# Pooled attention and a top-1 expert layer on one core: batches 1 to 3's keys turned in pairs, the loop's head left unaligned, half blocks' weights split in three parts

## The chip, the cores and the metric

The kernel runs on 1 core of a Trainium2 chip. The metric is the device time of one execution in microseconds (us). Of the kernel before, three timed runs are shown; the profile is of a fourth execution.

## The reference

```python
def _attn_ref(q, k, v):                      # 8 batches, 8 heads, 576 rows, 64 columns
    k_p = k.reshape(B, H, Sp, pool, D).mean(axis=3)      # 576 keys pooled by 8: 72
    v_p = v.reshape(B, H, Sp, pool, D).mean(axis=3)
    scores = scale * np.matmul(q, k_p.transpose(0, 1, 3, 2))
    ...
    return np.matmul(attn, v_p)              # attn: softmax of the scores

def _moe_ref(x, w_gate, w1, w2):             # x: 4608 tokens of 512, from attention
    expert_idx = np.argmax(x @ w_gate, axis=1)           # 8 experts, the best one
    ...
    for e in range(E):                       # w1[e]: 512 x 1024, w2[e]: 1024 x 512
        h = np.maximum(x_sorted[lo:hi] @ w1[e], 0.0)
        y_sorted[lo:hi] = h @ w2[e]
    return gate_w[:, None] * y_sorted[inv_perm]
```

## The kernel before

**Attention.** For each batch, keys and values are loaded as 5 chunks of 128 pooled rows x 512 columns (the fifth has 64 rows; the 512 are 8 neighbouring rows of 64). Three adds halve the columns to 512, 256, 128 and 64 (`pool`, L327; POOL's instructions are at L331, L333 and L335). PE turns the pooled keys (`k_pe`), and they are scaled into the tile `bd`, once in partitions 0 to 63 and once in 64 to 127 (`half`), since a query pair takes both halves of PE's rows. How the upper half is filled differs by batch. For batches 0 to 2 (`b < TWICE`) the last add is done on DVE and writes every chunk's 64 columns twice, side by side (`doubled`, L323; `kp` is then a part of the tile `both`), so that one turn gives both halves, and ACT copies the lower, DVE the upper (`two`, L383). From batch 3 on, POOL does the last add, PE turns 64 columns a chunk, ACT fills the lower half, and a DMA on SP's queue copies it to the upper (`moves`, issued at L1050). The queries are taken in 36 units; `put(i, place, step)` hangs steps into unit i at a named place, and each engine runs its steps in the order in which this program writes them. After every few units, tokens are routed: POOL scatters them by expert into the DRAM tensor `x_by_expert` (L691).

**Weights.** Each expert's float32 weights are split into a high and a low float16 part in eight pieces (0 to 3 of `w1`, 4 to 7 of `w2`): ACT rounds the high part (`wsplit`, L118), DVE makes the low part from both (L120). The first expert's pieces are split during units 12 to 32, the low parts of it in units 23 to 31.

**Expert loop.** Tokens go in blocks of up to 256 of one expert: 22 blocks with these inputs. Block 0 is done ahead of the loop; the loop runs blocks 1 to 21. A block of at most 128 rows runs half the columns (`full` false): blocks 4, 6, 11, 15 and 21. Its code is one of four copies of `block` (two weight buffers, full or half), chosen by branches in `either`. The body on PE: the products with w1 (`up_part`, `up`, L987 to L996), then those with w2 (`finish`, L1080), 24 products of 512 columns for each 128 rows. In the first block of an expert (`en` is 1: blocks 1, 4, 5, 7, 8, 12 and 15), ACT and DVE also split the next expert's eight pieces into the other weight buffer (`part`, L1277). Ahead of that stands `split_x` (L891): it splits a later block's rows, which the loop has loaded from `x_by_expert`, and waits for POOL's `keep_ids` (L872 to L877), which waits for these rows. SP's queue then runs `trans` (a DMA that turns the rows, L906), `load_x` (rows of the block three ahead, L1219) and `wwhole` (the weights of later experts, L91), in this order. The loop is written with PE's code for its head aligned to the start of a page of instructions (`head_align_engines=[ENG.PE]`).

## Time and profile before

| | us |
|---|---|
| median of 3 runs (lowest, highest) | 592.79 (590.35, 593.44) |
| the profiled execution | 594.33 |
| its span, first to last instruction | 592.5 |
| PE busy | 567.3 (96%) |
| DVE, ACT, POOL busy | 284.6, 277.9, 264.5 |

The profiled execution lies 1.54 us above the median. PE works through 96% of the span, so the table's other engines matter only where PE waits for one of them. Attention takes about the first 160 us; the loop begins at about 190. Rows give times in us from the span's start.

### The profile page before, as it was taken

What the parts mean: (1) busy time and instruction counts of PE and PEld (TensorE: products, weight loads), DVE (VectorE), ACT (ScalarE), POOL (GpSimd) and SP (SyncE); (2) the same over time, 40 slices, a digit from 0 to 9 for tenths busy, and PEclk for the clock granted to TensorE, in tenths of its full rate; (3) what the DMA queues carried; (4) which work ended last, traced back from release to release, by engine and by line L of the source; (5) the groups of instructions that cost most, each with busy time, mean ns of one, the idle gap of its engine ahead of it and who ended that gap; (6) DMA issues with size and microseconds to landing.
All of it is one profiled execution on the core that took longest, in us unless ns stands there. A gap on an engine that the chain in (4) does not pass through costs nothing. (4 is left out here: it accounts for less than half of the span.)

```text
span 592.5 us, 15080 instructions
## 1 busy us (share of the span) xinstructions
PE 567.3 (96%) x4384; PEld 422.6 (71%) x4385; DVE 284.6 (48%) x575; ACT 277.9 (47%) x625; POOL 264.5 (45%) x526
## 2 busy tenths in 40 slices
PE   8989899999998989998998999999999999999995
PEld 8888899989884765766674676676765667657763
DVE  6776466688864272228724751326512551133022
ACT  3767788889731262236735641236412642122122
POOL 5779989987964641133320433140420142201212
PEclk9999999999999999999999999999999999999998
DMA  9999998956694859636995888233142322420200
GB/s 268 300 311 287 333 327 257 318 215 203 186 307 151 236 139 394 225 90 190 270 309 112 298 253 280 53 95 82 45 111 57 83 69 85 111 59 32 71 18 34
DMA packets 96583, 107.61 MB, mean 182 GB/s; under 512 B 54502, under 2 KB 64742, under 8 KB 96552
## 3 DMA queue, kind: packets, MB, share of 16 engines
q1 hardware_dynamic: 89832, 85.93, 51.1%
q0 software_dynamic: 6720, 21.28, 9.4%
q8 instruction: 17, 0.28, 0.2%
q14 instruction: 14, 0.11, 0.1%
HBM read 73.65 MB, written 23.37 MB: 164 GB/s over the span
## 5 line engine op out<-in xcount | busy, mean ns | idle before, releaser
L1080 PEld LDWEIGHTS <-bd 128*128 128x128 f16 x936 | 91.3, 98 | 105.6
L1074 DVE SCALAR_TENSOR_TENSOR bd<-ps,bd 128x512 f16<-128x512 f32 (+1 forms) x44 | 27.6, 630 | 178.0 <-ACT bd L1071 173.7
L1242 POOL TENSOR_TENSOR spacer<-ql,iG 1x1 f32<-1x1 f32 x44 | 21.5, 489 | 188.8 <-ACT ql L1238 185.9
L515 ACT ACTIVATE both<-ps,nmx 128x72 f32<-128x72 f32 x288 | 69.1, 343 | 6.9 <-DVE nmx L508 6.7
L1071 ACT ACTIVATE bd<-ps 128x512 f16<-128x512 f32 (+1 forms) x44 | 24.1, 549 | 91.9 <-PE L996 66.0
L541 PE MATMUL po<-vb,pt 128*128 128x146 f32 (+3 forms) x400 | 57.7, 305 | 1.4 <-ACT pt L527 1.1
L1080 PE MATMUL po<-w,bd 128*128 128x512 f16 x264 | 58.9, 379 | 0.0
L1080 PE MATMUL po<-kv,bd 128*128 128x512 f16 x264 | 58.8, 379 | 0.0
L1243 POOL DMA_INDIRECT out_dram<-ql,iG x44 | 45.4, 1033 | 21.3 <-issue 20.2
L996 PEld LDWEIGHTS <-qt 128*128 128x128 f16 x528 | 47.7, 98 | 8.8 <-issue 1.8
L541 PEld LDWEIGHTS po<-vb,pt 128*128 128x128 f32 (+1 forms) x400 | 50.5, 177 | 4.8 <-ACT pt L527 3.3
L996 PEld LDWEIGHTS <-w 128*128 128x128 f16 x480 | 40.8, 98 | 14.9 <-ACT w L118 5.8
L1080 PE MATMUL pq<-kv,bd 128*128 128x512 f16 x216 | 48.1, 379 | 0.0
L498 PE MATMUL ps<-bd,qT 128*128 128x144 f32 x256 | 43.6, 294 | 4.1 <-ACT both L515 2.5
L1080 PE MATMUL pq<-w,bd 128*128 128x512 f16 x192 | 42.9, 379 | 0.0
L1238 ACT ACTIVATE ql<-po,gB 128x512 f32<-128x512 f32 x22 | 15.0, 684 | 57.1 <-PE L996 37.1
L691 POOL DMA_INDIRECT x_by_expert<-both,rpos x36 | 36.3, 1009 | 10.4 <-issue 4.9
L498 PEld LDWEIGHTS ps<-bd,qT 128*128 128x128 f32 x256 | 35.0, 190 | 6.0 <-ACT both L515 3.5
L508 DVE TENSOR_REDUCE nmx<-ps 128x4 f32<-128x288 f32 x72 | 32.0, 451 | 9.9 <-PE ps L498 9.6
L331 POOL TENSOR_TENSOR st<-kv 128x1280 f32<-128x1280 f32 x12 | 34.9, 2909 | 3.9 <-DMA kv<-in_k_dram 2.6
L895 DVE TENSOR_TENSOR bd<-vb,bd 128x1024 f16<-128x1024 f32 x22 | 27.0, 1225 | 20.1 <-issue 10.6
L527 ACT ACTIVATE pt<-pp 128x640 f32<-128x640 f32 x36 | 25.6, 710 | 20.3 <-PE pp L522 14.5
(244 smaller groups left out, 1190.3 us busy)
## 6 DMA issues: line engine op xcount, KB each, us to landing
both<-in_moe_w_dram SPq DMA_DIRECT2D x6, 2048.0 KB, 11.6
st<-in_moe_w_dram SPq DMA_DIRECT2D x6, 2048.0 KB
vb<-x_by_expert SPq DMA_DIRECT2D x16, 578.0 KB
kv<-in_v_dram SPq DMA_DIRECT2D x16, 512.0 KB
st<-in_moe_w_dram SPq DMA_DIRECT2D x8, 1024.0 KB
kv<-in_k_dram SPq DMA_DIRECT2D x6, 1024.0 KB
qt<-in_q_dram SPq DMA_DIRECT2D x6, 1024.0 KB
kv<-in_k_dram SPq DMA_DIRECT2D x4, 512.0 KB
```

Source lines behind the costliest of these rows:

```text
L331: nc.gpsimd.tensor_tensor(t1, src[:, :, 0:4 * D], src[:, :, 4 * D:], op=OP.add)
L498: nc.tensor.matmul(ps[:, x * 2 * KP:(x + 1) * 2 * KP], t[:, h, :], BD[b % 3][:, :, h, :], start=True, stop=True)
L508: nc.vector.tensor_reduce(nmx, ps[:, 0:4 * KP].rearrange("p (h x) -> p h x", x=KP), axis=AX.X, op=OP.min)
L515: nc.scalar.activation(p[:, PCOL[h]:PCOL[h] + KP], ps[:, x * KP:(x + 1) * KP], AF.Exp, bias=nmx[:, x:x + 1], scale=-1.0)
L527: nc.scalar.activation(pt, pp[:, 0:640], AF.Copy)
L541: nc.tensor.matmul(po.rearrange("p a x -> p (a x)")[m, cols], pt[:, c * 128 + m.start:c * 128 + m.stop], VB[(b + s) % 3][:, c, SLOTS[c][0] ...
L691: st = nc.gpsimd.indirect_dma_start(out=xs, out_offset=bass.IndirectOffsetOnAxis(ap=Z["pos"][:, u:u + 1], axis=0), in_=X[:, u, :], in_offs ...
L895: nc.vector.tensor_tensor(col(xh[:, :, 1]), row(xg), col(xh[:, :, 0]), op=OP.subtract)
L996: nc.tensor.matmul(dst, W1[s][z][:, d, c], xT[:, x, 0:n], start=(z == 0 and x == 0), stop=(z == 1 and d == DC - 1))
L1074: V.scalar_tensor_tensor(pair(hT[1], k, n), ups_of(k, n), 0.0, pair(hT[0], k, n), op0=OP.max, op1=OP.subtract)
L1080: nc.tensor.matmul(y, hT[x][:, f, 128 * j:128 * j + 128], W2[s][z][:, f, :], start=(half == x == z == f == 0), stop=(half == z == 1 and f ...
L1243: st = nc.gpsimd.indirect_dma_start(out=out, out_offset=bass.IndirectOffsetOnAxis(ap=iG[:, j:j + 1], axis=0), in_=ys[j], in_offset=None, b ...
```

## The change

It has four parts.

1. Keys. `kp` gets six chunk columns; the sixth is a copy of chunk 0. For batches 1 to 3, PE turns two neighbouring chunks at a time (`pair`): the lower 64 partitions of a result hold chunk c, the upper 64 chunk c+1. ACT copies the lower half to its columns, DVE the upper to columns that begin 128 further (`high`, 64x448), and the pair of chunk 4 and the copy gives the first 128. `doubled` goes: for batch 2, POOL does the last add; for batch 1, DVE does it in thirds, writing 64 columns instead of 128. Batch 3's DMA from half to half goes, and its last chunk is turned with the values (`v_pe`). For batches 2 to 7, POOL makes the copy (128x64).
2. The loop's head is no longer aligned on PE.
3. In half blocks, pieces 0 and 1 are split after the first half of the w1 products in program order, 2 and 3 after `arrive`, both ahead of `split_x`, and 4 to 7 behind it. Each of the three stands under an If of its own.
4. The low parts of the first expert's pieces are made in two DVE steps of 128x512 each, the second one place of the units later.

```diff
@@ -104,6 +104,15 @@
         nc.sync.dma_start(dst, src.rearrange("e p c f -> p (e c) f"))
 
     last_pool = []
+
+    def wsplit_low(s, i, z):
+        if i < 4:
+            c = slice(z * F // 2, (z + 1) * F // 2)
+            src, h, l = (x[..., c] for x in (ST[0][0][i // 2][:, i % 2, :], W1[s][0][:, i, :], W1[s][1][:, i, :]))
+        else:
+            j = 2 * (i - 4) + z
+            src, h, l = ST[0][1][j // 4][:, j % 4, :], W2[s][0][:, j, :], W2[s][1][:, j, :]
+        nc.vector.scalar_tensor_tensor(l, src, SW, h, op0=OP.mult, op1=OP.subtract)
 
     def wsplit(s, i, what="hl", stage=0):
         s1, s2 = ST[stage]
...
@@ -311,28 +320,29 @@
-    TWICE = 3
-
-    def pool_short(src, dst, twice=False):
+    TWICE = 4
+
+    def pool_short(src, dst, two_sums=False):
         for c in (slice(0, 2), slice(2, 4), slice(4, 5)):
             nc.gpsimd.tensor_tensor(t1[:, c], src[:, c, 0:4 * D], src[:, c, 4 * D:], op=OP.add)
-            nc.gpsimd.tensor_tensor((t3 if twice else t2)[:, c], t1[:, c, 0:2 * D], t1[:, c, 2 * D:], op=OP.add)
-            if not twice:
+            nc.gpsimd.tensor_tensor((t3 if two_sums else t2)[:, c], t1[:, c, 0:2 * D], t1[:, c, 2 * D:], op=OP.add)
+            if not two_sums:
                 nc.gpsimd.tensor_tensor(dst[:, c], t2[:, c, 0:D], t2[:, c, D:], op=OP.add)
 
-    def doubled(c=slice(0, 5)):
-        n = c.stop - c.start
-        nc.vector.tensor_tensor(kp[:, c], t3[:, c, None, 0:D].to_broadcast([128, n, 2, D]),
-                                t3[:, c, None, D:].to_broadcast([128, n, 2, D]), op=OP.add)
+    def thirds(c):
+        nc.vector.tensor_tensor(KVS["kp", 1][:, c], t3[:, c, 0:D], t3[:, c, D:], op=OP.add)
+        if c.start == 0:
+            nc.vector.tensor_tensor(KVS["kp", 1][:, 5], t3[:, 0, 0:D], t3[:, 0, D:], op=OP.add)
 
     def pool(src, dst, what=(0, 1)):
         last_pool[:] = []
         if 0 in what:
             nc.gpsimd.tensor_tensor(t1, src[:, :, 0:4 * D], src[:, :, 4 * D:], op=OP.add)
         if 1 in what:
-            nc.gpsimd.tensor_tensor(t3 if dst is kp else t2, t1[:, :, 0:2 * D], t1[:, :, 2 * D:], op=OP.add)
-            if dst is not kp:
-                nc.gpsimd.tensor_tensor(dst, t2[:, :, 0:D], t2[:, :, D:], op=OP.add)
+            nc.gpsimd.tensor_tensor(t2, t1[:, :, 0:2 * D], t1[:, :, 2 * D:], op=OP.add)
+            nc.gpsimd.tensor_tensor(dst[:, 0:5], t2[:, :, 0:D], t2[:, :, D:], op=OP.add)
+            if dst.shape[1] == 6:
+                nc.gpsimd.tensor_tensor(dst[:, 5], t2[:, 0, 0:D], t2[:, 0, D:], op=OP.add)
 
     def pool_now(src, dst, part):
         p1 = pbig[:, 0:1280].rearrange("p (c x) -> p c x", c=5)
...
@@ -348,10 +358,8 @@
     def pool_k(b, part):
-        if b < TWICE:
-            KVS["kp", b] = kp
-        elif part == 0:
-            KVS["kp", b] = work.tile([128, 5, D], F32, name="kp", bufs=2)
+        if part == 0:
+            KVS["kp", b] = work.tile([128, 6, D], F32, name="kp", bufs=2)
         pool(kv[(2 * b) % 3], KVS["kp", b], (part,))
...
@@ -362,38 +370,47 @@
     def half(b, s):
         return BD[b % 3][64 * s:64 * s + 64, s].rearrange("p h x -> p (h x)")
 
-    WITH_K = (1, 2, 3)
+    ALONE = (1, 2)
 
     def k_pe(b):
         kp = KVS["kp", b]
-        m = 128 if b < TWICE else 64
+        pm = KVS["pk", b] = psA.tile([128, 512], F32, name="pq", bufs=2)
+        if b >= TWICE:
+            for c in range(4):
+                nc.tensor.transpose(pm[0:64, c * 128:(c + 1) * 128], kp[:, c], ident)
+            return
+        for c in range(4):
+            pair(kp, c, pm[:, c * 128:(c + 1) * 128])
+        if b in ALONE:
+            KVS["p4", b] = psA.tile([128, 512], F32, name="pq", bufs=2)
+            pair(KVS.pop(("kp", b)), 4, KVS["p4", b][:, 0:128])
+
+    def pair(kp, c, pm):
+        nc.tensor.transpose(pm, kp[:, c:c + 2].rearrange("p c d -> p (c d)"), ident)
+
+    def low(b, cols, pm):
+        return nc.scalar.activation(half(b, 0)[:, cols], pm, AF.Copy, scale=-SC)
+
+    def high(b, cols, pm):
+        return nc.vector.tensor_scalar(half(b, 1)[:, cols], pm, -SC, None, op0=OP.mult)
+
+    def both_halves(a, d):
+        tc.declare_no_dep(d.ins, a.ins, reason="reads of other partitions")
+
+    def k_act(b):
+        pm = KVS.pop(("pk", b))
+        a = low(b, slice(0, 512), pm[0:64, 0:512])
         if b < TWICE:
-            kp = kp.rearrange("p c t d -> p c (t d)")
-        pm = KVS["pk", b] = psA.tile([128, 512], F32, name="pq", bufs=2)
-        for c in range(4):
-            nc.tensor.transpose(pm[0:m, c * 128:(c + 1) * 128], kp[:, c], ident)
-        if b in WITH_K:
-            k_last(b, kp, psA.tile([128, 512], F32, name="pq", bufs=2)[:, 0:64])
-            KVS.pop(("kp", b))
-
-    def k_last(b, kp, pm):
-        KVS["p4", b] = pm
-        nc.tensor.transpose(pm[0:128 if b < TWICE else 64], kp[0:64, 4], ident[0:64, 0:64])
-
-    def two(b, cols, pm, n):
-        a = nc.scalar.activation(half(b, 0)[:, cols], pm[0:64, 0:n], AF.Copy, scale=-SC)
+            both_halves(a, high(b, slice(128, 576), pm[64:128, 0:448]))
+        if b in ALONE:
+            k_last_act(b)
+
+    def k_last_act(b):
+        pm = KVS.pop(("p4", b))
+        a = low(b, slice(512, 576), pm[0:64, 0:64])
         if b < TWICE:
-            d = nc.vector.tensor_scalar(half(b, 1)[:, cols], pm[64:128, 0:n], -SC, None, op0=OP.mult)
-            tc.declare_no_dep(d.ins, a.ins, reason="reads of other partitions")
-
-    def k_act(b):
-        two(b, slice(0, 512), KVS.pop(("pk", b)), 512)
-        if b in WITH_K:
-            k_last_act(b)
-
-    def k_last_act(b):
-        two(b, slice(512, 576), KVS.pop(("p4", b)), 64)
-        if b >= TWICE:
+            both_halves(a, high(b, slice(0, 128), pm[64:128, 0:128]))
+        else:
             moves.append((half(b, 1), half(b, 0)))
 
     def v_pe(b):
...
@@ -403,12 +420,16 @@
-        if b and b not in WITH_K:
-            k_last(b, kp, pm[:, 384:448])
+        if b and b not in ALONE:
+            KVS["p4", b] = pm[:, 384:512]
+            if b < TWICE:
+                pair(kp, 4, pm[:, 384:512])
+            else:
+                nc.tensor.transpose(pm[0:64, 384:448], kp[0:64, 4], ident[0:64, 0:64])
     def v_act(b):
-        if b and b not in WITH_K:
+        if b and b not in ALONE:
             k_last_act(b)
...
@@ -797,10 +818,9 @@
-    KVS["kp", 1] = kp
-    pool_short(kv[2], kp, True)
+    pool_short(*pooled("kp", 1), True)
-    doubled(slice(0, 2))
+    thirds(slice(0, 2))
...
@@ -849,7 +869,6 @@
-                    put(4, "dve", doubled)
                     prep(b, (4, "2"), (5, "2"), (6, ""))
...
@@ -866,7 +885,8 @@
         put(*h, wsplit, 0, j, "h")
-        put(x, "dve2", wsplit, 0, j, "l")
+        put(x, "dve2", wsplit_low, 0, j, 0)
+        put(x + 1, "dve", wsplit_low, 0, j, 1)
...
@@ -1274,23 +1294,30 @@
     take(0)
     give(0)
 
-    def part(s, en):
+    def part(s, en, js=range(8)):
         with tc.If(en > 0):
-            for j in range(8):
+            for j in js:
                 wsplit(1 - s, j, "hl", s)
 
     def block(s, full, en):
         n = BLK if full else 128
         for f in range(0, FC, 2):
             up_part(s, f, n, 0)
+        if not full:
+            part(s, en, (0, 1))
         for k in range(4):
             up_part(s, 2 * k, n, 1)
             up(s, 2 * k + 1, n)
             relu_hi(k, n)
             relu_lo(k, n)
         arrive()
-        split_x()
-        part(s, en)
+        if full:
+            split_x()
+            part(s, en)
+        else:
+            part(s, en, (2, 3))
+            split_x()
+            part(s, en, (4, 5, 6, 7))
         if full:
             for half in range(2):
                 finish(s, 1, half)
...
@@ -1304,7 +1331,7 @@
-    with tc.For_i(0, T, 1, iteration_sync="reg_based", head_align_engines=[ENG.PE]) as t:
+    with tc.For_i(0, T, 1, iteration_sync="reg_based") as t:
```

On POOL, the third and the fourth batch's pooling (`kv_148` holds batch 2's keys, `kv_149` its values). Before:

```order
L331 TENSOR_TENSOR st_65<-kv_148 128x1280
L333 TENSOR_TENSOR st_64<-st_65 128x640
L331 TENSOR_TENSOR st_65<-kv_149 128x1280
L333 TENSOR_TENSOR st_65<-st_65 128x640
L335 TENSOR_TENSOR vp<-st_65 128x320
```

In the changed kernel:

```order
L340 TENSOR_TENSOR st_65<-kv_148 128x1280
L342 TENSOR_TENSOR st_65<-st_65 128x640
L343 TENSOR_TENSOR kp<-st_65 128x320
L345 TENSOR_TENSOR kp<-st_65 128x64
L340 TENSOR_TENSOR st_65<-kv_149 128x1280
L342 TENSOR_TENSOR st_65<-st_65 128x640
L343 TENSOR_TENSOR vp<-st_65 128x320
```

POOL does two instructions more for batch 2's keys ahead of its values: the last add and the copy.

On DVE, in the unit in which batch 2's keys are turned (`bd_156` takes them). Before:

```order
L508 TENSOR_REDUCE nmx<-ps 128x4 x2
L325 TENSOR_TENSOR both<-st_64 128x640
L572 TENSOR_SCALAR ri<-po 128x8
L574 RECIPROCAL ri<-ri 128x8
L576 TENSOR_TENSOR both<-po,ri 128x576
L508 TENSOR_REDUCE nmx<-ps 128x4
L386 TENSOR_SCALAR bd_156<-pq 64x512
L386 TENSOR_SCALAR bd_156<-pq 64x64
```

In the changed kernel:

```order
L529 TENSOR_REDUCE nmx<-ps 128x4 x2
L593 TENSOR_SCALAR ri<-po 128x8
L595 RECIPROCAL ri<-ri 128x8
L597 TENSOR_TENSOR both<-po,ri 128x576
L529 TENSOR_REDUCE nmx<-ps 128x4
L395 TENSOR_SCALAR bd_156<-pq 64x448
L395 TENSOR_SCALAR bd_156<-pq 64x128
```

The 128x640 add ahead of the copies into the upper half is gone; the copies have 448 and 128 columns instead of 512 and 64.

On ACT, in the loop's half block of the first weight buffer (`bd_154` takes the results of w1, `qt_150` and `kv_148` are the other buffer's high parts). Before:

```order
L1071 ACTIVATE bd_154<-pp 128x2x128
L1071 ISA
L1071 ACTIVATE bd_154<-pq 128x2x128
L892 ISA
L892 ACTIVATE bd_156<-vb_159 128x2x512
L1278 COMPARE_AND_BRANCH
L118 ISA
L118 ACTIVATE qt_150<-st_64 128x1024
L118 ISA
L118 ACTIVATE qt_150<-st_64 128x1024
L118 ISA
L118 ACTIVATE qt_150<-st_64 128x1024
```

In the changed kernel, at the block's start and further on:

```order
L1298 COMPARE_AND_BRANCH
L127 ACTIVATE qt_150<-st_64 128x1024
L127 ISA
L127 ACTIVATE qt_150<-st_64 128x1024
L1298 UNCONDITIONAL_BRANCH
L1298 REGISTER_ALU
L1298 UNCONDITIONAL_BRANCH
L1091 ISA
L1091 ACTIVATE bd_154<-ps 128x2x128
L1091 ISA
L1091 ACTIVATE bd_154<-ps 128x2x128
```

and

```order
L1091 ACTIVATE bd_154<-pq 128x2x128
L1298 COMPARE_AND_BRANCH
L127 ISA
L127 ACTIVATE qt_150<-st_64 128x1024
L127 ISA
L127 ACTIVATE qt_150<-st_64 128x1024
L1298 UNCONDITIONAL_BRANCH
L1298 REGISTER_ALU
L1298 UNCONDITIONAL_BRANCH
L912 ISA
L912 ACTIVATE bd_156<-vb_159 128x2x512
L1298 COMPARE_AND_BRANCH
```

The rounding of pieces 0 and 1 (L127) stands ahead of the block's first L1091, that of 2 and 3 between its last and the split of the rows (L912, before L892); the pieces of w2 are left behind it.

## Rows read from the trace of the kernel before

**Rows 1.** The page's parts 1 and 2: engines' busy time, and TensorE's granted clock by slice.
```profile
PE 567.3 (96%) x4384; PEld 422.6 (71%) x4385; DVE 284.6 (48%) x575; ACT 277.9 (47%) x625; POOL 264.5 (45%) x526
...
PEclk9999999999999999999999999999999999999998
```

**Rows 2.** Waits of PE over the span: line, released by, us in total, times, longest.
```profile
PE ps L498 <- DMA bd<-bd: 1.5, 1, 1.5
...
PE ps L996 <- ACT qt L118: 0.9, 2, 0.6
PE pq L654 <- ACT bd L384: 0.8, 1, 0.8
```

**Rows 3.** Timeline 37 to 45: start, us, engine, line, operation, tiles [idle before <-releaser].
```profile
37.58 2.90 POOL L331 TENSOR_TENSOR st<-kv 128x1280 f32<-128x1280 f32 x1 [1.24 <-DMA kv<-in_v_dram]
...
38.34 2.82 DVE L325 TENSOR_TENSOR both<-st 128x640 f32<-128x640 f32 x1
...
41.21 0.66 PE L374 MATMUL pq<-ident,both 128*128 128x128 f32 x4 [1.29 <-DVE both L325]
...
44.12 2.90 POOL L331 TENSOR_TENSOR st<-kv 128x1280 f32<-128x1280 f32 x1 [0.62 <-DMA kv<-in_k_dram]
```

**Rows 4.** By stretch: length, busy PE, PEld, DVE, ACT, POOL (count), clock, DMA share, GB/s.
```profile
67.00:131.00 64.00, 63.21 (x522) 58.99 (x521) 42.46 (x119) 51.49 (x174) 59.29 (x76) 1.00 0.85 286
```

**Rows 5.** Timeline of POOL, 86 to 110.
```profile
88.28 1.00 POOL L691 DMA_INDIRECT x_by_expert<-both,rpos  x1 [0.98 <-DVE ri L574]
...
107.79 0.86 POOL L335 TENSOR_TENSOR vp<-st 128x320 f32<-128x320 f32 x1
```

**Rows 6.** Timeline of PE, 108.5 to 111.
```profile
109.16 0.38 PE L403 MATMUL pq<-ident,vp 128*128 128x128 f32 x2
```

**Rows 7.** Waits of PE, 123 to 164.
```profile
PE ps L498 <- ACT both L515: 1.0, 2, 0.5
PE po L541 <- ACT pt L527: 0.9, 2, 0.7
```

**Rows 8.** Timeline of DVE, 123 to 150.5.
```profile
124.52 2.67 DVE L120 SCALAR_TENSOR_TENSOR w<-st,w 128x1024 f16<-128x1024 f32 x1
...
150.35 1.22 DVE L120 SCALAR_TENSOR_TENSOR w<-st,w 128x1024 f16<-128x1024 f32 x1
```

**Rows 9.** Timeline of PE where the loop is entered and where its first turn ends.
```profile
191.55 1.14 PE L996 MATMUL ps<-kv,w 128*128 128x256 f16 x9 [1.67 <-issue]
...
214.08 1.91 PE L996 MATMUL ps<-kv,w 128*128 128x256 f16 x16 [1.53 <-ACT kv L118]
```

**Rows 10.** DMA queues, 188 to 216: q8 carries PE's instructions.
```profile
q8 instruction: 4, 0.07, 1.1%
```

**Rows 11.** DMA queues, 215 to 580: all that moved anything.
```profile
q1 hardware_dynamic: 50944, 43.34, 42.3%
q0 software_dynamic: 3200, 8.70, 6.3%
```

**Rows 12.** Waits of PE, 261 to 300 (block 5 begins in it).
```profile
PE ps L996 <- ACT w L118: 1.9, 4, 0.6
```

**Rows 13.** Timeline 261 to 277: the end of block 4, the start of block 5.
```profile
262.93 0.19 POOL L872 TENSOR_TENSOR gC<-vb,zf 128x2 f32<-128x2 f32 x1 [3.58 <-DMA vb<-x_by_expert]
...
267.10 9.17 DVE L120 SCALAR_TENSOR_TENSOR w<-both,w 128x1024 f16<-128x1024 f32 x8
...
273.98 2.34 POOL L1242 TENSOR_TENSOR spacer<-ql,iG 1x1 f32<-1x1 f32 x1 [9.21 <-ACT ql L1238]
```

**Rows 14.** Waits of PE, 300 to 330 (block 8 begins in it).
```profile
PE ps L996 <- ACT w L118: 1.5, 3, 0.6
```

**Rows 15.** Timeline 311 to 325: the end of block 7, the start of block 8.
```profile
300.78 10.30 SPq L906 DMA_TRANSPOSE kv<-bd  x1
...
317.74 0.19 POOL L872 TENSOR_TENSOR gC<-vb,zf 128x2 f32<-128x2 f32 x1 [8.80 <-DMA vb<-x_by_expert]
...
318.92 1.06 ACT L892 ACTIVATE bd<-vb 128x1024 f16<-128x1024 f32 x1 [7.20 <-POOL vb L877]
```

More of the change, by code (lines that the diff above doesn't have):

```diff
@@ L764 @@
     turned((0, 1))
-    two(0, slice(0, H * KP), pm, H * KP)
+    both_halves(low(0, slice(0, H * KP), pm[0:64, 0:H * KP]), high(0, slice(0, H * KP), pm[64:128, 0:H * KP]))
     g_qt(0, 1)
```

8 lines of the change are left out of this document (4 added, 4 removed).

## The prediction

> **What bounds the kernel now.** I read the page first. PE is busy for 567.3 us of a span of 592.5, at a granted clock of full speed (2.4 GHz) in all slices but the last [rows 1]. So the kernel is PE's work plus some 25 us in which PE stands, and an edit that leaves PE's work alone can only gain from these. Next I read PE's waits, over the whole span and by stretch, and then the timeline around each wait, to see what is late behind what PE waits for. That second question decides this case, because a wait that goes gives time at the end only if nothing else holds PE later.
>
> The waits that the change aims at are these. In attention, PE waits 1.29 us for DVE's 128x640 add of batch 2's keys [rows 3], 0.8 us for ACT's copy of a last key chunk and 1.5 us for the DMA that copies batch 3's keys from half to half [rows 2]; together 3.6. From 123 to 164 us it waits 1.0 us for the exponentials (L515) and 0.9 us for copies (L527), while DVE makes low weight parts [rows 7]. At the loop's entry it stands 1.67 us, waiting for nothing that the trace shows, and 1.53 us where the first turn ends [rows 9]. At the start of block 5 it waits 1.9 us in four steps for the splitting of the weights [rows 12], at block 8 1.5 us in three [rows 14], at block 16 0.9 us in two [rows 2].
>
> **The keys.** The three waits go: batch 2's add moves to POOL, batch 3's DMA is not issued, and its last chunk moves to the turn with the values. PE turns as much as before. But POOL is the next in line. It starts batch 3's keys at 44.12, when their load lands, which an earlier PE doesn't bring forward [rows 3], and from 67 to 131 it is busy 59.29 of 64 us [rows 4]. It ends batch 6's values at 107.79 + 0.86 = 108.65, and PE takes them at 109.16 [rows 5, 6]. There is no slack: however early PE comes to this place, it waits for POOL. So I cost the 3.6 us at nothing. On POOL the change adds the copy of 128x64. The trace has none behind batch 2; bounds are the smallest add, 0.19 us for 128x2 [rows 13], and the 128x320 add, 0.86 [rows 5]. Between them by columns it is 0.19 + 64/320 x 0.67 = 0.32, an estimate. Four copies (keys 3 to 6) stand ahead of those values: 1.3 us, from 0.8 to 3.4. Against that, POOL idles 0.98 us at 88.28 for DVE [rows 5], which runs behind PE; with PE earlier this idle goes. Sum: **+0.3** (from -0.2 to +2.4). Batch 2's own additional add (0.86) and copy fit into the 1.24 us in which POOL waits for a load at 37.58 [rows 3].
>
> **The low parts in two steps.** A 128x1024 low part takes 1.22 us; the first took 2.67, beside POOL's adds [rows 8]. What PE needs next stands behind it on DVE. Halved, a step holds the queue about half as long. The waits that this can touch are 1.9 us [rows 7]; I take **-1.2**, since the ACT waits of 0.9 may have ACT's own queue behind them. Ends: -1.9, and +1.5 if eight more starts cost the 0.19 us of the smallest operation each and all lie on the path.
>
> **The head.** Ahead of the entry PE's instruction queue fetches code: four of its fetches lie between 188 and 216 us [rows 10], around the two stops [rows 9]. Without the alignment the head starts within a page, the first branch's target lies nearer to it, and I expect the 1.67 to go and the 1.53 to stay, whose jump is as far as before.
>
> **Half blocks.** Pieces 0 to 3 of the next weights are split before the rows, so the waits at blocks 5 (1.9) and 16 (0.9) go. Block 7 is a full block; its order is unchanged, and block 8's wait stays.
>
> What do 1.67 and 1.9 bring? Block 8 waits for pieces that ACT rounds after `split_x`, which waited 7.20 us for POOL, which waited 8.80 us for the rows of a load [rows 15]. That load stood behind a turning DMA that took 10.30 us, queued behind 4 MB of weights [rows 15]. The same chain of loads, turns and weights goes back to the table of blocks, made before the loop is entered, and is paced by transfers. PE's early gains only lengthen its wait at block 8. I cost the **entry and block 5 at nothing**. Behind block 8 no such chain is left, and PE's only waits to the end are those of block 16: **-0.9**.
>
> The edit also delays the chain. In block 4 two low parts (9.17 / 8 = 1.15 us each [rows 13]) now stand on DVE just when the rows land, at 262.93, and POOL has to clear their ids. POOL's tiny add beside DVE's chain of eight took 2.34 us and ended, at 276.32, when the chain ended at 276.27 [rows 13]. If DVE comes earlier because PE does, less of that overlaps; and the weights behind it are free a little sooner, as fewer pieces are left after the rows. I take **+0.5**, between 0 and 2.3 (both low parts in full).
>
> *Sum:* +0.3 - 1.2 + 0 + 0 - 0.9 + 0.5 = -1.3 us against the profiled execution's 594.33, that is 593.0. This execution lies 1.54 above the median, so against 592.79 it is **591.5**. From no change the measurement can tell about 0.5%, 3.0 us: below 589.8 is faster, above 595.8 slower. With its unknowns the forecast's own range is 590.0 to 593.8.
>
> **Two rules against the rows.** POOL's 2.34 us shows that it stood through the rest of a chain of eight DVE operations [rows 13]. The Trainium skill (SBUF — State Buffer, Who interferes with whom) has it that VectorE with two SBUF inputs and a reading GpSimd share a lock that is held for one whole instruction, which by itself would let POOL in after 1.15 us at most; by that the delay would be at most 1.2, and the sum no worse than -0.6. The row speaks for the longer hold, so I keep 2.3 as the end.
>
> From 215 to 580 us only the two data queues moved anything [rows 11]: no instruction was fetched in twenty turns of a loop that branches among four copies of its block. The Trainium skill (Runtime: NRT & Kernel Launch, Instruction fetch mechanics) says that a taken branch out of the two 16 KiB pages at hand makes the engine fetch its target. By that rule every turn would have paid, aligned or not; the trace disagrees.
>
> **Rivals.**
>
> *POOL doesn't hold PE (0.15).* The 3.6 us are kept, if POOL, freed of waits like that at 88.28, runs ahead. Against it: 93% busy [rows 4]. The sum is then -1.3 - 0.3 - 3.6 = -5.2: 587.6.
>
> *The chain of rows moves with PE (0.15).* Its steps in blocks 5 and 6 run behind relus that PE paces, so it may come forward. Then 1.67 and 1.9 are kept and the delay goes: -1.3 - 0.5 - 3.6 = -5.4: 587.4. Against it: the 10.30 and 8.80 us [rows 15], which an earlier start only lengthens. Both of these together, 0.02, give 583.5.
>
> *Slower: DVE's low parts hold up the rows (0.13).* Place: block 4, POOL's ids and with them ACT's split of the rows. Price: 2.3 in place of 0.5, and if also the two-step low parts bring nothing, -1.3 + 1.8 + 1.2 = +1.7: 594.5. It decides if DVE reaches pieces 2 and 3 at or after 262.9, that is if PE has not come earlier by then.
>
> *Slower: code that no longer stays (0.05).* The body's PE code, begun within a page, can touch one page more. If that one is fetched anew in each of 20 turns at 1.6 us [rows 9], it costs 32 us: 625. By the rule of the Trainium skill above, some such fetch is what a turn does. [Rows 11] speak against it. That the head's edit does nothing is possible too (one in five), but hardly moves the sum.
>
> **How the numbers follow.** The forecast has 0.50, the rivals 0.15, 0.15, 0.02, 0.13 and 0.05. Faster takes the two middle rivals but for a little, their joint case and the forecast's low tail: 0.31. Slower is the code's 0.05 and the upper tail of the delay: 0.07. Same has 0.62. The range from 587.0 to 595.0 leaves out the code, the joint case and the lower parts of the two faster rivals, 0.18 in all; at the top it takes in the delay.
>
> **What would show it.** Right: no DVE wait at batch 2's keys and no DMA wait at batch 3's; PE waiting for values near 110 us; the stop at the entry gone and that at the first turn's end there; no wait for weights at blocks 5 and 16; and at block 8 a wait of 5 us or more in place of 1.5, with PE's first product of block 8 within 1.5 us of where it was. Wrong: block 8 starting 4 us or more earlier (a faster rival), the rows of block 4 split 2 us later, or instruction fetches within the loop.

## The result, and the profile after

| | before | after |
|---|---|---|
| median (lowest to highest), us | 592.75 (590.35 to 593.44), 4 runs | 599.59 (599.45 to 604.78), 4 runs |
| ratio to before, 95% interval | | 1.0135 [1.0087, 1.0182] |
| the profiled execution, its span | 594.33, 592.5 | 599.56, 597.8 |

The changed kernel is slower by 6.8 us, where 591.5 was forecast. A second measurement, on the chip of the last experiments, gave 1.0119 [1.0067, 1.0171].

The page's engine row and clock row answer to [rows 1]:

```profile
PE 570.0 (95%) x4384; PEld 425.7 (71%) x4385; DVE 282.6 (47%) x585; ACT 276.8 (46%) x625; POOL 266.9 (45%) x533
...
PEclk9999999999999999988999999999999999999998
```

PE does the same 4384 products, and is busy 2.7 us longer: in two slices the granted clock is no longer full. Its waits over the span (line, released by, us in total, times, longest) answer to [rows 2]:

```profile
PE ps L1016 <- ACT ql L1258: 4.1, 1, 4.1
PE po L1100 <- ACT bd L1091: 3.2, 1, 3.2
PE pq L676 <- POOL rc L656: 2.6, 1, 2.6
```

The first two are new, and both belong to block 4. To see where time went I laid the start of each marked ACT step (the softmax units, the copies of the outputs, the splits of the rows) beside the same step of before. After minus before, in us: -1.79 at unit 5, +1.53 at unit 9, -0.21 at unit 11, -0.31 when the table of blocks is made, -1.92 in block 2, **+6.45 in block 8**, +5.22 from block 16 to the end. So all of the loss arises between about 206 and 330 us, and attention is even.

**Attention.** Two timelines show it, POOL's and PE's; the first rows answer to [rows 3, 5]:

```profile
44.59 2.90 POOL L340 TENSOR_TENSOR st<-kv 128x1280 f32<-128x1280 f32 x1 [1.16 <-DMA kv<-in_k_dram]
...
55.73 0.20 POOL L656 TENSOR_TENSOR rc<-cum,zf 128x8 f16<-128x8 f32 x1
...
109.55 0.44 PE L420 MATMUL pq<-ident,vp 128*128 128x128 f32 x2 [0.44 <-POOL vp L343]
```

The three waits for keys are gone, and PE reaches unit 5 1.79 us sooner. Then it waits 2.6 us for a small routing step of POOL that ends at 55.93; before it ended at 55.19. POOL got its load 0.47 us later and makes a copy of 0.32 more. The rest of the stop is PE's own lead. Behind it the granted clock falls, where before had 1.00 (window of after: length, busy PE, PEld, DVE, ACT, POOL, clock, DMA share, GB/s):

```profile
58.00:60.00 2.00, 2.00 (x11) 1.80 (x9) 0.80 (x3) 1.80 (x7) 2.00 (x3) 0.50 1.06 222
```

Four products that took 0.60 us before (L471, now L492) take 1.06 in it. PE left the stop 0.19 us ahead of before (56.14 for 56.33) and was 1.53 behind by unit 9; the DMA wait of 1.5 us that is gone at 66 us only brought the marker back to -0.21. So the first two waits were lost to POOL, and the third to the clock behind that stop. The second stop for POOL, forecast near 110 us, is there too.

**The loop.** First the timeline of before, the rows that stood in no group: the fourth low part of block 1, the turn of the rows on SP's queue, the landing of block 3's rows (POOL), and the w2 products of block 4.

```profile
208.82 4.62 DVE L120 SCALAR_TENSOR_TENSOR qt<-st,qt 128x1024 f16<-128x1024 f32 x4
...
209.06 3.04 SPq L906 DMA_TRANSPOSE kv<-bd  x1
...
249.84 0.19 POOL L872 TENSOR_TENSOR gC<-vb,zf 128x2 f32<-128x2 f32 x1 [11.34 <-DMA vb<-x_by_expert]
...
261.11 5.34 PE L1080 MATMUL po<-kv,bd 128*128 128x512 f16 x24
...
264.62 1.06 ACT L892 ACTIVATE bd<-vb 128x1024 f16<-128x1024 f32 x1 [1.73 <-POOL vb L877]
```

The same places in the timeline of after, as far as the end of block 4:

```profile
208.26 4.62 DVE L129 SCALAR_TENSOR_TENSOR qt<-st,qt 128x1024 f16<-128x1024 f32 x4
...
213.26 1.83 SPq L926 DMA_TRANSPOSE kv<-bd  x1
...
254.15 0.19 POOL L892 TENSOR_TENSOR gC<-vb,zf 128x2 f32<-128x2 f32 x1 [17.56 <-DMA vb<-x_by_expert]
...
258.09 1.89 PE L1016 MATMUL ps<-kv,qt 128*128 128x128 f16 x16 [4.10 <-ACT ql L1258]
...
266.34 2.00 ACT L127 ACTIVATE w<-both 128x1024 f16<-128x1024 f32 x2 [8.36 <-SPq L1352]
...
267.67 1.09 POOL L892 TENSOR_TENSOR gC<-vb,zf 128x2 f32<-128x2 f32 x1 [5.69 <-DMA vb<-x_by_expert]
268.72 1.18 POOL L893 TENSOR_TENSOR iC<-vb,zi 128x2 int32<-128x2 int32 x1
269.98 0.20 POOL L897 TENSOR_TENSOR vb<-far,zi 128x2 int32<-128x2 int32 x1
...
267.49 2.36 DVE L129 SCALAR_TENSOR_TENSOR w<-both,w 128x1024 f16<-128x1024 f32 x2 [9.60 <-ACT w L127]
...
268.67 7.04 PE L1100 MATMUL po<-kv,bd 128*128 128x512 f16 x24 [3.24 <-ACT bd L1091]
...
271.20 1.08 ACT L912 ACTIVATE bd<-vb 128x1024 f16<-128x1024 f32 x1
```

Read in order of time:

1. *The turn is late in block 1, a full block, whose own order is unchanged.* The rows were split on DVE by 208.33 (before 208.91), but the turn is issued at 213.26, right behind the fourth low part (208.26 + 4.62 = 212.88). Before it was issued at 209.06, behind the rows.
2. *The lateness is handed on.* Block 3's rows land 4.3 us later (254.15), ACT splits them with its copies of the outputs queued behind, and PE stops 4.10 us ahead of block 4.
3. *Block 4's relus are held.* ACT's first two pieces wait until 266.34 for SP's queue to come past the weights' place at the end of its turn (L1352); SP comes there behind the late turn and `load_x`. The relus stand behind them on ACT, and PE stops another 3.24 us.
4. *Block 4's own rows are held.* They land 4.7 us late (267.67 for 262.93), and are split 6.6 us late (271.20 for 264.62): another 1.9 us is lost inside the block. POOL's two tiny adds take 1.09 and 1.18 us in place of 0.19 and 0.20, beside DVE's low parts of pieces 0 and 1 (267.49), which are late themselves. POOL is through at 270.18, though, and ACT, with pieces 2 and 3 ahead of the split, begins it only at 271.20. Before, the split began 0.56 us behind POOL; by that it could have begun at 270.74 here, so POOL alone would account for some 1.4 us of the 1.9 and ACT's order for the rest, an estimate.

Each of POOL's adds stood as long as one low part (1.18). The Trainium skill (SBUF — State Buffer, Who interferes with whom) has it that the ports which the two engines share are an exclusive lock and that, in VectorE's two-port modes, whoever issues first has them for the whole instruction; the length of these two waits agrees with that, where the 2.34 us of [rows 13] was longer.

SP's waits of 186 to 330 us name the first link:

```profile
SPq L926 <- DVE qt L129: 12.9, 2, 7.0
```

Before, SP waited there for the rows (`DVE bd L895`). TensorE's granted clock falls behind the stops. The windows of 5 us from 255 to 275, in the same columns:

```profile
255.00:260.00 5.00, 1.91 (x19) 1.67 (x20) 1.23 (x1) 2.33 (x3) 1.96 (x5) 0.85 0.10 20
260.00:265.00 5.00, 5.00 (x76) 5.00 (x75) 0.00 (x0) 0.00 (x0) 1.63 (x5) 0.81 0.80 187
265.00:270.00 5.00, 1.76 (x12) 0.77 (x10) 2.51 (x3) 3.66 (x7) 2.25 (x3) 0.87 0.23 59
270.00:275.00 5.00, 5.00 (x20) 2.08 (x19) 5.00 (x8) 5.00 (x7) 0.37 (x2) 0.78 0.00 0
```

Before, all four had 1.00; these are mixtures of the two levels, 1.2 and 2.4 GHz. The 24 products took 7.04 us for 5.34, and block 4's w1 part, 258.09 to 265.43, took 7.3 us for 5.5 (255.75 to 261.28). At block 8 the late chain arrives (timeline, answering to [rows 15]):

```profile
308.54 9.00 SPq L926 DMA_TRANSPOSE kv<-bd  x1
...
324.20 0.19 POOL L892 TENSOR_TENSOR gC<-vb,zf 128x2 f32<-128x2 f32 x1 [11.85 <-DMA vb<-x_by_expert]
...
325.37 1.06 ACT L912 ACTIVATE bd<-vb 128x1024 f16<-128x1024 f32 x1 [7.00 <-POOL vb L897]
...
329.22 0.81 PE L1016 MATMUL ps<-kv,w 128*128 128x256 f16 x6 [1.29 <-DVE w L129]
```

The turn is 7.8 us later than before, the rows 6.5, the split 6.45, and this offset stays. A balance of PE from the loop's entry to block 8: new are 4.10 + 3.24 of stops and 1.7 + 1.8 at a lower clock; gone are 1.67 at the entry and 1.9 at block 5. That is +7.3, beside the +6.8 that the markers show (from -0.31 to +6.45).

**Why a full block's turn waits for low parts.** `trans` stands behind the branches, so one instruction of SP serves all four copies of the block, and its wait is one number: how many instructions an engine must have done in this turn. The program's own values, before and after:

```
before  SP, turn of the rows: DVE count 20, ACT count 20
after   SP, turn of the rows: DVE count 24, ACT count 24
```

In a half block the rows' split now comes four pieces later, so the count has to be 24 there; in a full block, where the rows' split is still the twentieth, 24 is the fourth piece. This is the theory that the experiments test, under the name of counts. Its rivals: the new order inside the half blocks (3 and 4 of the list), and the other three parts of the change.

### The profile page after: what moved, and what is told of

The parts are those of the page before. It is cut to its first block, busy times and chain, and to the rows that moved or that the text cites. A ratio compares the mean times of both kernels' runs of the same rounds, so it can differ in the third digit from the quotient of the medians.

```text
span 597.8 us, 15112 instructions
## 1 busy us (share of the span) xinstructions
PE 570.0 (95%) x4384; PEld 425.7 (71%) x4385; DVE 282.6 (47%) x585; ACT 276.8 (46%) x625; POOL 266.9 (45%) x533
## 4 chain that ended last, share of the span: by engine, by line
PE 53%; ACT 1%; issue 0%; ACTq 0%; POOLq 0%; POOL 0%
PE po L1100 16%; PE pq L1100 11%; PE ps L1016 7%; PE pq L1016 3%; PE pp L1016 3%; PE ps L1009 2%; PE ps L1007 2%; PE ps L1008 2%; PE pq L1007 1%; PE pp L1008 1%; PE pp L1007 1%; PE pq L1009 1%; PE pq L1008 1%; PE pp L1009 1%; ACT w L127 0%
## 5 line engine op out<-in xcount | busy, mean ns | idle before, releaser
L1262 POOL TENSOR_TENSOR spacer<-ql,iG 1x1 f32<-1x1 f32 x44 | 23.5, 535 | 185.2 <-ACT ql L1258 182.8
L1091 ACT ACTIVATE bd<-ps 128x512 f16<-128x512 f32 (+1 forms) x44 | 23.8, 547 | 88.2 <-PE L1016 78.9
L1100 PE MATMUL po<-kv,bd 128*128 128x512 f16 x264 | 60.5, 387 | 3.2 <-ACT bd L1091 3.2
L1016 PEld LDWEIGHTS <-qt 128*128 128x128 f16 x528 | 49.5, 101 | 11.9 <-issue 4.8
L912 ACT ACTIVATE bd<-vb 128x1024 f16<-128x1024 f32 x22 | 23.4, 1064 | 30.7 <-POOL vb L897 28.0
L1016 PE MATMUL ps<-kv,qt 128*128 128x256 f16 (+1 forms) x264 | 32.7, 268 | 4.1 <-ACT ql L1258 4.1
```

The costliest lines, as they stand in the source:

```text
L1016: nc.tensor.matmul(dst, W1[s][z][:, d, c], xT[:, x, 0:n], start=(z == 0 and x == 0), stop=(z == 1 and d == DC - 1))
L1100: nc.tensor.matmul(y, hT[x][:, f, 128 * j:128 * j + 128], W2[s][z][:, f, :], start=(half == x == z == f == 0), stop=(half == z == 1 and f ...
```

## The experiments

All ratios are to before on the same chip, with 95% intervals.

**The parts apart.** `c_only` is before with the half blocks' order alone (`part` with a list of pieces, as in the change); `no_c` and `no_c_again` are the changed kernel without it; `keys_low` is before with the keys and the two-step low parts, the head aligned; `head_only` is before with

```diff
-    with tc.For_i(0, T, 1, iteration_sync="reg_based", head_align_engines=[ENG.PE]) as t:
+    with tc.For_i(0, T, 1, iteration_sync="reg_based") as t:
```

> The kernel before with the half blocks' new order alone. Theory (counts): the turning DMA of the loop waits for one count of DVE's instructions that must hold in all four copies of the block; with four low parts ahead of the rows' split in the half copies, the full copies' DMA is held until their fourth low part is done. So in the loop's first turn it starts near 213 us, 4 us later than before, the rows of later blocks land about 4 us later, and block 4's relus stand behind pieces 0 and 1 on ACT, which wait for SP's queue to end its turn. Time: +6 to +7, 599. Rival (POOL kept out by low parts in block 4): the first turn's DMA where it was, rows of block 4 split up to 2.3 us later, 593 to 595. Rival (keys, head or low parts of attention cause the loss): 592 to 593.

> The changed kernel with the half blocks' order of before: keys, head and two-step low parts alone. Theory (counts): no late DMA, no wait at the relus; the gain of 1 us that the trace of the changed kernel shows at the loop's entry is kept, and perhaps the entry's stop: 590 to 592. Rival (POOL kept out): the same. Rival (keys, head or low parts cause the loss): 597 to 600.

> The changed kernel with the half blocks' order of before once more. In the first such run its span was 0.4 us under that of the kernel before in the median, its time 1.8 above, because 4.3 us of the time lay outside the span, against 2.0 for the kernel before. If that belongs to this program, it is 4.3 again, and the time 594.5 to 595.5; if to the place in the series of runs, it may change.

> The changed kernel with the loop's head aligned and the half blocks' order of before: keys and two-step low parts alone. PE is up to 2 us early until about 105 us, then waits for POOL; the low parts give 0.5 to 1 us by 165. Span 0.5 to 1.5 us under before. Rival (POOL does not hold PE): 3.5 us or more under it. Whether the 4.3 us outside the span stay with this program or with the one without alignment is not foreseen by any of these.

> The kernel before without the alignment of the loop's head. PE's stop at the entry (1.7 us) goes; the one at the end of the first turn stays, or grows, since the weights' low parts end at the same time; block 8 waits that much longer. Span within 0.7 us of before. Rival (early gains reach the end): 1.5 us under it.

| | us (before) | ratio |
|---|---|---|
| c_only | 599.69 (593.33) | 1.0124 [1.0041, 1.0206] |
| no_c | 595.10 (593.33) | 1.0037 [1.0013, 1.0061] |
| no_c_again | 595.02 (593.87) | 1.0009 [0.9975, 1.0043] |
| keys_low | 596.46 (594.33) | 1.0043 [1.0015, 1.0072] |
| head_only | 593.88 (594.33) | 1.0010 [0.9972, 1.0048] |

The half blocks' order alone gives the loss. In the timeline of `c_only` the turn is as late, and PE stops behind block 4's relus:

```profile
215.44 1.96 SPq L906 DMA_TRANSPOSE kv<-bd  x1
...
269.29 7.60 PE L1080 MATMUL po<-kv,bd 128*128 128x512 f16 x24 [4.34 <-ACT bd L1071]
```

(In this execution the block of the first turn ran 1.8 us later than in the profile before, so the turn's own lateness is 4.5.) The three other parts together change the span by nothing: the medians of the spans are 590.8 and 590.6 in the two runs, 591.1 and 590.9 in before. Their time is still 1 to 2 us above, for a reason told under the last heading. `head_only` is the same as before: the 1.67 us at the entry are gone, and PE stops longer where the first turn ends (waits of PE up to 215 us):

```profile
PE ps L996 <- ACT kv L118: 2.3, 1, 2.3
```

In `keys_low` PE waits for POOL as in after, and behind this stop the clock falls to 0.50 (56 to 58 us); that is where the keys' gain goes (waits of PE up to 215 us):

```profile
PE pq L676 <- POOL rc L656: 2.1, 1, 2.1
```

The two-step low parts bring nothing that can be seen: from 123 to 164 us PE waits 2.5 us in all in `keys_low` and 2.7 in `no_c`, for 2.4 before. After had 1.3 there, but 2.5 in its second profile, `after_5`. The time expected of `no_c` (590 to 592) and the span expected of `keys_low` (0.5 to 1.5 us under before) didn't come: 595.1, and 0.3 under.

**The count by itself.** No piece is moved; in half blocks four operations of one element on ACT and on DVE stand ahead of the rows' split, in full ones at the block's end.

```diff
+    def blanks(n):
+        for _ in range(n):
+            nc.scalar.activation(pada, zf[0:1, 0:1], AF.Copy)
+            nc.vector.memset(padv, 0.0)
...
+        if not full:
+            blanks(4)
         split_x()
         part(s, en)
+        if full:
+            blanks(4)
```

> The kernel before; no weight piece moves. In half blocks four operations on a single element stand ahead of the split of the rows on ACT and on DVE, in full blocks the same four stand at the end, so that the totals are equal. They compute nothing that is used. Theory (counts): the DMA that turns the rows again waits in full blocks for the fourth low part (213 us in the first turn, 4 us late) though nothing was moved; the span grows by 3 to 5 us. Any theory by which the moved pieces themselves cost the time (POOL kept out, relus held): the DMA at 209, no change beyond 0.5 us.

605.31 (593.87), 1.0196 [1.0119, 1.0272]. The turn (SP's timeline) comes at 215.90; the split of block 1's rows was 2.3 us later than in the profile before, so 4.5 of the 6.8 are the count's.

```profile
215.90 2.02 SPq L908 DMA_TRANSPOSE kv<-bd  x1
```

Its waits (186 to 330 us) name the low parts:

```profile
SPq L908 <- DVE qt L120: 15.0, 2, 8.6
```

So a count alone, with no piece moved, makes the turn as late as the change does. It costs time too: PE's w2 products lie 2.6 us behind before's in block 4, and 6.9 in block 5, where PE waits for pieces that ACT splits behind the late rows. But the span was expected to grow by 3 to 5 us and grew by 12 (medians), and not all of that is the turn's. At block 8 the lag goes from 7.3 to 11.15 us, and there PE's own wait has moved. Before (timelines of ACT and PE):

```profile
319.88 7.67 ACT L118 ACTIVATE w<-both 128x1024 f16<-128x1024 f32 x8
...
321.93 0.39 PE L996 MATMUL ps<-kv,w 128*128 128x256 f16 x2 [0.43 <-ACT w L118]
```

In `count_only`:

```profile
325.59 7.67 ACT L118 ACTIVATE w<-both 128x1024 f16<-128x1024 f32 x8
...
330.47 0.39 PE L998 MATMUL ps<-kv,w 128*128 128x256 f16 x2 [1.90 <-ACT w L118]
```

At 0.96 us a piece, PE's first stop ends behind the second piece before, and behind the fifth here: the blanks shift the count that PE waits for as well. So the experiment shows that the count makes the turn late, and that this costs some 4 us at block 5; its whole loss is that of two shifted counts.

**Which engine's count.** `c_highs_first` puts only the high halves of pieces 0 to 3 early; ACT's count moves, DVE's doesn't (shown against `c_only`):

```diff
-            part(s, en, (0, 1))
+            part(s, en, [(0, "h"), (1, "h")])
...
-            part(s, en, (2, 3))
+            part(s, en, [(2, "h"), (3, "h")])
             split_x()
-            part(s, en, (4, 5, 6, 7))
+            part(s, en, [(j, "l") for j in range(4)] + [(j, "hl") for j in range(4, 8)])
```

> The kernel before; half blocks round the high parts of pieces 0 to 3 in the change's places, all low parts come behind the split of the rows. Theory (counts): DVE's count is as before, but the DMA waits for ACT's count too, and in full blocks this now stands at the fourth high part: near 211 us in the first turn, 2 us late instead of 4. Pieces 0 and 1 still wait for the end of SP's turn and hold block 4's relus. 593 to 595. Rival (POOL kept out by low parts): 592 or less, no late DMA.

600.99 (593.33), 1.0139 [1.0079, 1.0199]. The turn comes at 210.62, between the others (timeline):

```profile
210.62 1.96 SPq L906 DMA_TRANSPOSE kv<-bd  x1
```

SP's waits (186 to 330 us) now name ACT's high parts too:

```profile
SPq L906 <- ACT qt L118: 4.1, 2, 2.1
```

The place was forecast within half a microsecond; the time wasn't (593 to 595). The relus are still held (`PE po L1080 <- ACT bd L1071`, 3.5 us), and 4.1 to 5.3 us of each execution lie outside the span, where `c_only` has 1.8: by the medians of the spans, of four executions each, it lies some 1.5 us under `c_only`.

**The counts made equal.** `c_pad`: pieces 0 to 3 stay ahead of the rows' split in half blocks (behind the relus); full blocks get four one-element operations there, half blocks at their end (shown against `c_only`, in part).

```diff
         if full:
+            for _ in range(4):
+                nc.scalar.activation(pada, zf[0:1, 0:1], AF.Copy)
+                nc.vector.memset(padv, 0.0)
             split_x()
             part(s, en)
...
```

> The kernel before with pieces 0 to 3 of half blocks ahead of the split of the rows (behind the relus), and four operations on a single element ahead of that split in full blocks, at the end in half blocks; they compute nothing that is used. The counts of both kinds of block are then equal. Theory (counts): the DMA is back at 209 us in the first turn; the span is within 1.5 us of before (block 4's rows split 1 to 2 us later, the waits at blocks 5 and 16 gone), 3 us under the same order without these operations. If the moved pieces themselves cost the time: 3 us over before.

604.26 (593.87), 1.0192 [1.0125, 1.026]. The turn is back in its place, and the rows of block 8 are split 0.4 us sooner than in before, 6.9 sooner than in after: the late chain is cured. But the span, expected within 1.5 us of before, is 10.8 above it (medians): PE now waits for the pieces where blocks 5 and 16 begin, blocks whose waits the order had removed. The timeline of `c_pad`, the turn, ACT's first four pieces and block 5:

```profile
207.86 3.15 SPq L908 DMA_TRANSPOSE kv<-bd  x1
...
260.88 3.90 ACT L118 ACTIVATE w<-both 128x1024 f16<-128x1024 f32 x4
...
267.10 3.88 ACT L118 ACTIVATE w<-both 128x1024 f16<-128x1024 f32 x4
...
268.19 0.61 PE L998 MATMUL ps<-kv,w 128*128 128x256 f16 x2 [3.07 <-ACT w L118]
```

And PE's waits from 186 us on, for block 16:

```profile
PE ps L998 <- DVE qt L120: 3.7, 2, 2.0
```

The blanks shift PE's count in turn, since PE waits for the pieces of an earlier turn by one number, whichever copy ran them: the first four pieces were rounded by 264.78, yet PE's stop at 268.19 ends behind the fifth, which began at 267.10. `no_c_pad2` puts two pieces ahead of the split and two blanks in their places, on the changed kernel:

> The changed kernel with only pieces 0 and 1 of half blocks ahead of the split of the rows, behind the relus, and two operations on a single element in each block that make the counts equal; they compute nothing that is used. Theory (counts): no late DMA, waits at block 5 halved, that at block 16 gone: span 589 to 591, 7 us under the changed kernel, and the best so far by a little. Rival: 593 or more.

597.77 (593.87), 1.0075 [1.0047, 1.0103]: not faster either, and 5 us above the span that was expected; PE's first stop at block 5 is 2.8 us.

**The relus set free.** `c_lows_first` (on before) and `after_s1` (on after) put pieces 0 to 3 between `arrive` and `split_x`, none ahead of the relus (shown against `c_only` and after):

```diff
-        if not full:
-            part(s, en, (0, 1))
...
-            part(s, en, (2, 3))
+            part(s, en, (0, 1, 2, 3))
             split_x()
```

> The kernel before; half blocks split pieces 0 to 3 behind the arrival of the rows of the next block and ahead of the split of the later rows, none ahead of the relus. Theory (counts): the DMA of full blocks still waits for the fourth low part (near 213 us in the first turn), the relus of block 4 wait for nothing new: 595 to 598, with PE's wait for the take of block 3's results still there and that for block 4's relus gone. Rival (POOL kept out): 593 to 595, no late DMA at 213.

> The changed kernel with pieces 0 and 1 of a half block moved from ahead of the relus to behind them, beside 2 and 3, so still ahead of split_x; trans stays behind the branches. If the relus held by the pieces' wait for the weights are most of the loss, 594 to 596; if the late rows are, 598 to 602, with PE's stop behind block 4's relus (3.2 us in the changed kernel) gone and the stop ahead of block 4 (4.1 us) still there.

598.31 (593.33), 1.0104 [1.0041, 1.0167], and 602.77 (594.74), 1.0141 [1.0063, 1.0219]. In both, the stop behind the relus is gone; the one ahead of block 4 is 0.25 and 1.61 us (1.42 in `c_only`, 1.60 in `after_5`), and PE now stops 2.0 us at the start of block 5, for ACT, which has gone on to the late rows ahead of the pieces that PE needs. From the timeline of `after_s1`:

```profile
267.03 1.23 POOL L892 TENSOR_TENSOR gC<-vb,zf 128x2 f32<-128x2 f32 x1 [5.54 <-DMA vb<-x_by_expert]
...
272.20 1.27 PE L1016 MATMUL ps<-kv,w 128*128 128x256 f16 x10 [2.02 <-ACT bd L912]
```

With the relus free, the late rows hold PE one step further on. In time little or nothing comes back. In spans (medians) `after_s1` has 598.3 us for 598.0 of `after_5`, but `c_lows_first` 594.0 for 597.9 of `c_only`, so that on the kernel before more than half of the order's 6.8 us is gone; its time hides that, with 4.2 to 4.4 us outside the span.

**The turn inside each copy.** `trans_in` and `trans_in_5` (the same kernel, twice) issue the turn in the copies, so that each has its own count; `trans_in_s1` also sets the relus free; `b_trans_in` is before with the turn inside and nothing else, the control. SP then also reads which copy runs.

```diff
-    def block(s, full, en):
+    def block(s, full, en, more):
...
             part(s, en, (4, 5, 6, 7))
+        with tc.If(more > 0):
+            trans()
...
-        with tc.If(more[0] > 0):
-            trans()
```

> The changed kernel, with the DMA that turns the rows issued inside each of the four copies of the block, so that in a full copy it waits for that copy's own count. Theory (counts): in the first turn it starts near 209 us again instead of 213, the rows of later blocks land 3 to 4 us earlier than in the changed kernel, and PE's 4.1 us wait ahead of block 4 goes. Pieces 0 and 1 still wait on ACT for the end of SP's turn and hold block 4's relus, 2 to 3 us. Span 592 to 595, 3 to 5 us under the changed kernel. If the late DMA were not the cause, no change: 597 to 598.

> The same with pieces 0 to 3 of half blocks all behind the relus, ahead of the split of the rows. Theory (counts): the wait for block 4's relus goes as well; the rows of block 4 are split 1 to 2 us late, the waits at blocks 5 and 16 are gone or small. Span 589.5 to 592, level with the kernel without the half blocks' order or a little under it. If the held relus cost nothing: as the run before.

> The kernel before, with its order of work unchanged, and SP's trans issued inside each of the four copies of a block in place of behind the branches. It is the control of the runs with trans inside: what the other place costs by itself. Theory of the counts: before, the count common to the copies fell on instructions that no copy reached late, so there is nothing to gain; 591 to 595 if SP's longer branch is free. Rival: SP's code inside the copies itself costs the 8 us that the changed kernel with trans inside lay above before: 599 to 603 with nothing else changed, and then that run says nothing against the theory of the late transfer.

> The changed kernel with trans inside each copy, again, in five rounds on the same chip as its control and as the changed kernel. If the late transfer of the rows (4 us at block 4) were most of the loss, this is 3 us or more below the changed kernel; if the order of the half blocks itself (block 4's own rows split 2 to 4 us late, the relus held by the first pieces) is most of it, it is within 2 us of it, or above.

> The changed kernel again, in five rounds on the same chip as the three others: 598 to 603, 1.2% or so above before.

| | us (before) | ratio |
|---|---|---|
| trans_in | 602.43 (594.33) | 1.0115 [1.0071, 1.0160] |
| trans_in_s1 | 602.61 (594.33) | 1.0121 [1.0065, 1.0177] |
| b_trans_in | 597.19 (594.74) | 1.0055 [1.0013, 1.0097] |
| trans_in_5 | 599.94 (594.74) | 1.0104 [1.0051, 1.0158] |
| after_5 | 600.27 (594.74) | 1.0119 [1.0067, 1.0171] |

The spans expected of `trans_in` (592 to 595) and `trans_in_s1` (589.5 to 592) didn't come: their medians are 600.1 and 600.4.

In `trans_in_5` the turn comes at 210.50 with a first block 1.4 us late, so on time, and the stop ahead of block 4 is 0.93 in place of 4.10. But the first pieces still wait for SP's mark, the relus behind them, and PE behind these (timeline):

```profile
264.16 2.00 ACT L127 ACTIVATE w<-both 128x1024 f16<-128x1024 f32 x2 [8.63 <-SPq L1352]
...
266.49 7.98 PE L1100 MATMUL po<-kv,bd 128*128 128x512 f16 x24 [5.01 <-ACT bd L1091]
...
269.02 1.08 ACT L912 ACTIVATE bd<-vb 128x1024 f16<-128x1024 f32 x1
```

So with the turn on time the new order still holds the relus and splits block 4's rows 4.4 us late (269.02 for 264.62; 3.0 of it beyond the late first block). How long PE stops at either place differs from one execution to the next: `trans_in`, the same kernel, has no stop ahead of block 4 and 1.96 us behind the relus, and `after_5` has 1.60 and 4.71 where after has 4.10 and 3.24. The control's place isn't free in time: 1.0055. Against its control, `trans_in_5` loses some 2.8 us (599.94 less 597.19), after 5.5 against before (600.27 less 594.74); that would put about half of the loss on the late turn and half on the order inside the half block, but the intervals overlap, and the control's profile lost its time in attention, ahead of anything that was edited, and none in the loop. I take the direction from the traces and leave the split open.

## Why the prediction was wrong

**Right.** The three waits for keys went and gave nothing in the end: POOL holds PE, at 55.73 already, and again at 109.55 where it was forecast; what the third gave back went to the lower clock behind the first of these stops, which the prediction doesn't have. The head's stop went, and the one at the first turn's end stayed (1.47 us). From 215 to 580 us the two data queues were again all that moved: no code was fetched in the loop, so the rival on code didn't come. (That the fetches of [rows 10] are PE's is an inference; no view names the engine of a queue.) At blocks 5 and 16 PE's waits went. Block 16's gain, forecast at -0.9, is the step from +6.45 to +5.22: -1.2.

**Near by luck.** Attention was forecast at -0.9, and the table of blocks was made 0.31 us sooner. The terms don't hold one by one. The -1.2 of the two-step low parts shows in this one profile (PE's waits from 123 to 164 us fell from 2.4 to 1.3 us) and not in `after_5`, `keys_low` or `no_c` (2.5, 2.5 and 2.7).

**Wrong.** The step that failed reads: "The edit also delays the chain ... I take +0.5, between 0 and 2.3 (both low parts in full)." From the table of blocks to block 8 it was +6.8. A delay such as this step described is there: 1.9 us more between the landing and the split of block 4's rows, with POOL standing 2.27 us beside two low parts. But it was not the rival's pair: DVE made the low parts of pieces 0 and 1 there, held late by ACT, and pieces 2 and 3, which the rival names, ended last on ACT and not on DVE. What the step left out is the part that costs more:

- *The turn's wait.* The step costed what is queued behind the moved pieces in the half block, and no wait of another queue. SP's turn waits for a number that all copies share. So the edit of half blocks delays the turn in block 1, a full one, by 4.2 us, and every transfer queued behind it. [Rows 15] showed that the chain is paced by transfers; I used that to argue that PE's gains end there, and not to ask what the edit does to the queue itself.
- *The pieces' wait.* I moved two pieces ahead of the relus without asking what they wait for. They wait for SP to reach the weights in the last turn (8.36 us on ACT), and relus with no part in this wait stand behind them: 3.24 us on PE, 4.71 in `after_5`, and 5.01 and 1.96 in the two profiles with the turn on time.
- *The clock.* A price of PE's stops beyond their length wasn't in the sum: some 3.5 us in block 4 at less than full clock.

The forecast that PE would merely wait 5 us or more at block 8 was wrong in the same way: the chain there is late by itself, and PE came late to it, with stops of 1.5 us in all.

**Open.** How the loss divides between the late turn and the order of the half block. Each costs something alone: with no piece moved, the late rows cost some 4 us at block 5 of `count_only`, and with the turn moved inside, the order still cost some 2.8 us beyond the control, by medians whose intervals overlap. Curing one gave back at most 1.4 us of time; in spans, `c_lows_first` gave back 3.9. No version was clearly faster than before.

## What to carry to other kernels

Where one instruction behind branches waits on a semaphore for all branch copies, its count is that of the latest copy: reordering one copy can delay the transfer in the others, and the number in the wait shows it before anything is run. Before moving work earlier on an in-order engine, look up what that work itself waits for; if it is another queue's progress, everything behind it inherits the wait. Operations that are put in only to make one count equal can shift others, as `count_only` and `c_pad` show. And a wait removed at one block is a gain only if the chain that feeds the next stop isn't touched by the same edit.

## What was not expected of the hardware

Stops of PE were followed by stretches at a lower granted clock: 0.78 to 0.87 in the windows of after at block 4, and in `trans_in_5` behind its 5.01 us (windows):

```profile
263.00:268.00 5.00, 1.51 (x4) 0.59 (x5) 2.69 (x4) 3.84 (x7) 2.55 (x3) 0.70 0.17 52
268.00:273.00 5.00, 5.00 (x15) 1.86 (x14) 5.00 (x9) 5.00 (x7) 0.19 (x1) 0.62 0.00 0
```

The 24 products then took 7.98 us, 2.6 more than at full clock. In `c_pad`, behind its 3.07 us, two products of block 5 took 0.61 us, and 0.39 in before. The length of a stop doesn't decide alone. The four short stops of 1.9 us in all at block 5 of before [rows 12] left the clock at 1.00; four of 2.1 us at the same place in `no_c` were followed by this window:

```profile
271.00:273.00 2.00, 2.00 (x13) 1.43 (x12) 2.00 (x3) 2.00 (x3) 0.00 (x0) 0.59 0.11 9
```

In attention, the 2.64 us behind POOL in after were followed by 0.50, and 3.20 us at the same place in `after_5` by 1.00 throughout. No run shows what decides it. By the two stretches of block 4 (1.7 and 1.8 us in the balance above), a profile of one execution can lose some 1.7 us by such a stretch alone.

Second, what an execution takes outside its span differs by program: 4.2 to 4.6 us in all ten executions of `keys_low` and 4.0 to 4.6 in all twenty of `no_c` and `no_c_again`, but 1.8 to 3.5 in those of before and 1.8 in all four of `c_only`. That is why a span equal to before's gave 1 to 2 us more in time. It comes neither with the keys nor with the order alone: `c_lows_first` had 4.2 to 4.4 and `c_highs_first` 4.1 to 5.3, after 1.8 to 3.4. No run shows its cause.
